# Channel attention into a SwiGLU block: one set of q and k buffers, five of six pairs of d_ff tiles by 7 products, the gate product cut in two, batch 1's softmax spread out

## The chip, the cores and the metric

The kernel runs on one core of a Trainium2 chip. The metric is the device time of one execution in microseconds (us), the median of the runs. The core has five engines that work side by side: TensorE (PE in the profile; its weight loads are PEld), VectorE (DVE), ScalarE (ACT), GpSimd (POOL) and SyncE (SP), which here only issues DMA transfers. Each works through its own instructions in the order in which they were written. A profile was taken of one execution.

## The reference

```python
def _attn_ref(q, k, v, tau):                 # q, k, v: (2, 6016, 256) fp32
    qn = q / (np.linalg.norm(q, axis=1, keepdims=True) + 1e-06)
    kn = k / (np.linalg.norm(k, axis=1, keepdims=True) + 1e-06)
    s = kn.transpose(0, 2, 1) @ qn / tau     # (2, 256, 256)
    s = s - s.max(-1, keepdims=True)
    a = np.exp(s)
    a /= a.sum(-1, keepdims=True) + 1e-09
    return v @ a

def _moe_ref(x, w_gate, w_val, w_out, rms_g):    # x: (12032, 256); weights fp64; d_ff = 1536
    rms = np.sqrt(np.mean(x * x, axis=-1, keepdims=True) + 1e-06)
    xn = x / rms * rms_g
    g = xn @ w_gate
    silu = g * (1.0 / (1.0 + np.exp(-g)))
    val = xn @ w_val
    return silu * val @ w_out
```

The result of the attention, both batches one below the other, is the x of the second function.

## The kernel before

Rows are worked on in tiles of 128. A batch has 47 of them. `scores` multiplies k's tile by q's for the 256 x 256 score matrix; `squares` (ScalarE) squares both, `add_squares` (VectorE) adds the squares up in `acc`, and at the end `join_squares` and `norm_sums` make the column norms of it. Batch 0 goes through this first, chunk by chunk. The `raw` pool holds the chunks of q and k: for batch 0 four buffers of 4 tiles, then, in a pool opened anew, five buffers of 2 tiles for batch 1's 24 chunks. `load_qk` issues two transfers for a chunk on SP, as soon as the chunk that had the buffer before has been squared.

After batch 0's softmax come 24 blocks of up to 4 row tiles, 512 rows (blocks 11 and 23 have 3 tiles, 384 rows; blocks 0 to 11 are batch 0's, 12 to 23 batch 1's). A block j runs through 12 steps f, one for each tile of d_ff, 128 wide; the text writes (j, f) for a step. Every fp32 operand is kept as a high and a low part, and a product is three matmuls: high by high, high by low, low by high.

- A **plain** step (`emit_hidden`) makes gate and value of one d_ff tile with 12 matmuls of 512 columns: six for the gate (`pg`), six for the value (`pv`). ScalarE takes the sigmoid (L629), VectorE multiplies it by the gate (L632, which frees the gate's PSUM bank) and by the value (L639).
- A step by **7 products** (`emit_pair`) works on a pair p = f // 2 of d_ff tiles: halves of the rows and of the 256 inputs are combined as in Strassen's scheme, and one half of the pair's hidden values comes from 7 products of 3 matmuls of 256 columns, 21 in all. The 7 products stand in four PSUM banks. ScalarE copies the first (L580), VectorE adds up the others (L588 to L591). The second step of a pair then takes the sigmoid of both gates (L585, ScalarE), multiplies it by the gates on GpSimd (L586, 1024 columns) and by the values there too (L600, twice 512 columns).

Either way the hidden values are then rounded to a high part on ScalarE (`run_rounds`, L539) and their low part is a subtraction (`run_subs`, L545): on GpSimd for a plain tile, on VectorE for a pair. `emit_out` multiplies the hidden tile by w_out, two steps later in blocks 0 and 1 and three later from block 2 on: 12 matmuls of 256 columns (po) that close each step on TensorE. All products share four PSUM banks (the pool `ps_gv`).

Blocks 0 and 1 are plain throughout (`WINO = 2`). From block 2 on the pairs in `PLAIN` are plain and the others go by 7 products:

```python
PLAIN = (0, 4)
SP = [p for p in range(NP) if p not in PLAIN]
```

Block 0 does two more things. Its steps decode the fp64 weights into fp32 (`decode_w`, `split_w`, three operations of 768 columns a tile on VectorE), and they are filled up with batch 1's scores and squares (`fill`, `square`, `add`; the function `more` calls them with 2 chunks in steps 0 to 4, 1 in the others). `end_block_0` closes that and makes batch 1's norms. Block 1 builds the combined weights for the 7 products (`build_s`, three pieces for a pair, all in the pair's second step).

While block j runs, the activations of block j + 1 are made in its steps, by the table `ready`: v's pieces are transposed in step 0 and split in step 1, multiplied by the softmax in steps 2 and 3, normalized in 4 and 5; at the end of step 5 `emit_xT_move` transposes in VectorE and issues 16 transfers on SP that complete the transposition; `emit_xT_parts` in step 8 scales what lands (L476, ScalarE) and makes the sums for the 7 products (L482, VectorE), and `emit_xT_round` in steps 9 and 10 rounds them (L492). Within a step the order on each engine is the order of the code: the step's own work, then `ready`, then `extra`, the list that `at(j, f, ...)` fills. Batch 1's softmax stands in `extra` at steps 5 to 9 of block 10:

```python
at(B1 - 2, 5 + i, go)
```

## Time and profile before

| | |
|---|---|
| median of 3 runs | 1377.85 us (1377.44 to 1380.14) |
| profiled execution | 1377.68 us, span 1375.9 us |
| mean granted clock of TensorE | 0.981 of full speed |
| TensorE busy | 1322.1 us (96%), 9420 matmuls |
| VectorE busy | 1013.4 us (74%) |
| ScalarE busy | 645.9 us (47%) |
| GpSimd busy | 677.2 us (49%) |

The span is the profiled execution from its first to its last recorded instruction. Busy times are sums over the whole span, whose stages differ: batch 0's scores, the softmax between the phases, block 0 with its extra work, block 1, and the blocks after them.

### The profile page before, as it was taken

The page shows a single profiled execution, that of the slowest core. Times are in us where ns is not written, and L with a number is a line of the kernel's source. Part 1 is how long each engine was busy: PE and PEld are TensorE (multiplying, and loading weights), DVE is VectorE, ACT ScalarE, POOL GpSimd, SP SyncE. Part 2 cuts the span into 40 slices and gives each one's busy share as a digit, 9 for nine tenths or more (in the row PEclk, how much of TensorE's full clock was granted, in tenths as well). Part 3 has the DMA queues.
Part 4 walks back from the last instruction along what each step waited for, and adds up shares of the span by engine and source line. Part 5 has one row for each costly group of instructions (what it writes and reads, how often), then busy time and mean ns, then how long its engine had stood idle before and what let it go on. Part 6 is the DMA issues. An engine that isn't in the chain of part 4 may idle for free.

```text
span 1375.9 us, 24750 instructions
## 1 busy us (share of the span) xinstructions
PE 1322.1 (96%) x9420; PEld 1244.3 (90%) x9420; DVE 1013.4 (74%) x1597; ACT 645.9 (47%) x1244; POOL 677.2 (49%) x500
## 2 busy tenths in 40 slices
...
DMA packets 150870, 71.61 MB, mean 52 GB/s; under 512 B 109280, under 2 KB 136928, under 8 KB 150752
## 3 DMA queue, kind: packets, MB, share of 16 engines
...
q8 instruction: 74, 1.21, 0.4%
...
## 4 chain that ended last, share of the span: by engine, by line
PE 85%; DVE 7%; DMA 2%; ACT 2%; issue 1%; SPq 1%; POOL 0%; DVEq 0%; ACTq 0%; POOLq 0%
PE p L568 31%; PE po L659 26%; PE pg L618 9%; PE pv L618 9%; PE s L175 5%; PE px L377 5%; DMA raw<-in_k_dram 2%; DVE acc L197 1%; DVE wx L120 1%; DVE hh L639 1%; SPq L461 1%; DVE wk L521 1%; DVE th L632 0%; ACT sq L188 0%; DMA raw<-in_q_dram 0%
## 5 line engine op out<-in xcount | busy, mean ns | idle before, releaser
L659 PE MATMUL po<-w,gh 128*128 128x256 f32 x2256 | 409.3, 280 | 0.7 <-ACT gh L539 0.7
L659 PEld LDWEIGHTS po<-w,gh 128*128 128x128 f32 x2256 | 352.1, 188 | 10.0 <-ACT gh L539 1.1
L586 POOL TENSOR_TENSOR th<-th,z 128x1024 f32<-128x1024 f32 (+1 forms) x88 | 207.2, 2354 | 226.4 <-ACT th L585 225.9
L659 PE MATMUL po<-w,gl 128*128 128x256 f32 x1128 | 314.9, 279 | 1.4 <-DVE gl L545 1.4
L568 PE MATMUL p<-xt,w 128*128 128x256 f32 (+1 forms) x2112 | 311.2, 282 | 4.8 <-DVE z L632 4.1
L568 PEld LDWEIGHTS p<-xt,w 128*128 128x128 f32 x2112 | 276.5, 190 | 5.9 <-DVE z L632 4.5
L545 POOL TENSOR_TENSOR gl<-z,gh 128x512 fp32r<-128x512 f32 (+1 forms) x88 | 119.3, 1355 | 240.8 <-ACT gh L539 230.1
L600 POOL TENSOR_TENSOR z<-th,z 128x512 f32<-128x512 f32 (+1 forms) x176 | 220.1, 1272 | 12.2 <-DVE z L591 6.9
L568 PE MATMUL p<-xt,s 128*128 128x256 f32 (+1 forms) x1584 | 217.9, 282 | 2.6 <-DVE z L632 2.3
L659 PEld LDWEIGHTS po<-w,gl 128*128 128x128 f32 x1128 | 212.1, 188 | 1.8 <-DVE gl L545 1.8
L539 ACT ACTIVATE gh<-z 128x512 fp32r<-128x512 f32 (+1 forms) x264 | 163.3, 619 | 88.3 <-POOL z L600 78.5
L568 PEld LDWEIGHTS p<-xt,s 128*128 128x128 f32 x1584 | 200.0, 189 | 4.0 <-DVE z L632 3.2
L588 DVE TENSOR_TENSOR z<-p,z 128x512 f32<-128x512 f32 (+1 forms) x176 | 119.4, 678 | 105.2 <-PE p L568 102.0
L618 PE MATMUL pg<-xt,w 128*128 128x512 f32 (+1 forms) x672 | 178.4, 401 | 4.3 <-DVE th L632 3.5
L618 PE MATMUL pv<-xt,w 128*128 128x512 f32 (+1 forms) x672 | 173.4, 393 | 0.0
L580 ACT ACTIVATE z<-p 128x256 f32<-128x256 f32 (+1 forms) x176 | 66.7, 379 | 201.2 <-PE p L568 197.2
L618 PEld LDWEIGHTS pv<-xt,w 128*128 128x128 f32 x672 | 126.9, 189 | 29.4
L618 PEld LDWEIGHTS pg<-xt,w 128*128 128x128 f32 x672 | 120.2, 190 | 26.4 <-DVE th L632 4.8
L591 DVE TENSOR_TENSOR z<-p,z 128x512 f32<-128x512 f32 (+1 forms) x176 | 119.6, 680 | 19.4 <-DVE z L590 1.4
L589 DVE TENSOR_TENSOR z<-p,z 128x512 f32<-128x512 f32 (+1 forms) x176 | 119.6, 680 | 18.3
L629 ACT ACTIVATE z<-pg 128x512 f32<-128x512 f32 (+1 forms) x88 | 51.4, 584 | 161.9 <-PE pg L618 161.3
L545 DVE TENSOR_TENSOR gl<-z,gh 128x512 fp32r<-128x512 f32 (+1 forms) x176 | 117.8, 702 | 5.9 <-ACT gh L539 5.0
...
## 6 DMA issues: line engine op xcount, KB each, us to landing
...
```

Source lines behind the costliest of these rows:

```text
L175: nc.tensor.matmul(out=s_ps[b][:, c, :], lhsT=r[:, 1, t, c * P:(c + 1) * P], rhs=r[:, 0, t, :], start=(t0 + t == 0 and c == 0), stop=(t0 + ...
L377: nc.tensor.matmul(out=px[:, i, :], lhsT=w[:, c, t * P:(t + 1) * P], rhs=x[:, c, :], start=(i == 0 and c == 0 and m == 0), stop=(c == KC - ...
L539: nc.scalar.activation(out=gh, in_=hh, func=AF.Copy)
L545: engine.tensor_tensor(out=gl, in0=hh, in1=f32(gh), op=ALU.subtract)
L568: nc.tensor.matmul(out=t[:, i, :h], lhsT=wm[wi], rhs=xm[xi], start=(i == 0 and q == 0), stop=(q == 2), skip_group_check=True,)
L586: nc.gpsimd.tensor_tensor(out=th[:, :2 * n], in0=th[:, :2 * n], in1=zg[:, :2 * n], op=ALU.mult)
L588: nc.vector.tensor_tensor(out=zz[:, 0:5:4], in0=ps[1], in1=twice(zz[:, 3:4]), op=ALU.add)
L589: nc.vector.tensor_tensor(out=zz[:, 1:3], in0=ps[2], in1=twice(zz[:, 4:5]), op=ALU.add)
L591: nc.vector.tensor_tensor(out=zz[:, 1:3], in0=ps[3], in1=zz[:, 1:3], op=ALU.add)
L600: nc.gpsimd.tensor_tensor(out=o, in0=i0, in1=i1, op=ALU.mult)
L618: nc.tensor.matmul(out=t[:, :n], lhsT=wgv[wi][:, f, c, wj, :], rhs=x[xi][:, c, :n], start=(m == 0), stop=(m == 3 * KC - 1),)
L659: nc.tensor.matmul(out=o_ps[j][t // 2][:, t % 2, :], lhsT=g[:, t * P:(t + 1) * P], rhs=wo[w][:, f, :], start=(f == 0 and t % 2 == 0 and m ...
```

## The change

- **Buffers.** One `raw` pool of three 4-tile buffers serves both batches; batch 1 comes in 11 chunks of 4 tiles and one of 3. `seq` lists all chunks, and `load_next` issues the next one wherever a chunk has been used up. Batch 1's scores and squares go by parts of 2 tiles; the square of a chunk's second part is written to the output buffer `ob`. The `h` buffers of the plain blocks are one of each instead of two. A step of block 0 fills 2 parts when f is odd, 1 when it is even.
- **Pairs.** `PLAIN = (5,)`: one pair is plain, the last, instead of the first and the fifth. The combined weights of five pairs are built, three pieces one step apart; the first sums of each (two of 512 columns) go to GpSimd.
- **Gate product.** GpSimd's product of 1024 columns is two of 512.
- **Batch 1's norms and softmax.** The end of the sums moves from (0, 11) to (1, 0) and (1, 1), the softmax from steps 5 to 9 of block 10 to single steps of blocks 4 to 7 and two of block 10. v's load for block 1 moves behind step 0 of block 0.

```diff
-    PLAIN = (0, 4)
+    PLAIN = (5,)
...
-    for b, sizes in enumerate(([2] + [4] * 9 + [2] * 4 + [1], [2] * 23 + [1])):
+    for b, sizes in enumerate(([2] + [4] * 9 + [2] * 4 + [1], [CH] * 11 + [3])):
...
-    def squares(b, i):
-
-        n = chunks[b][i][1]
-        sq = pool["sq"].tile([P, 2, n, C], F32, tag="sq", name=f"sq_{b}_{i}")
-        nc.scalar.activation(out=sq, in_=raw[b, i], func=AF.Square)
+    def squares(b, i, t=0, n=None):
+
+        n = n or chunks[b][i][1]
+
+        p, tag = (o_p, "ob") if b and t else (pool["sq"], "sq")
+        sq = p.tile([P, 2, n, C], F32, tag=tag, name=f"sq_{b}_{i}_{t}")
+        nc.scalar.activation(out=sq, in_=raw[b, i][:, :, t:t + n, :], func=AF.Square)
         return sq
...
-        at = [[wgv[0][:, f, c].rearrange("p j m -> p (j m)") for c in range(KC)] for f in (f0, f1)]
         if piece == 0:
-            t = pool["wk"].tile([P, 8, 2 * P], F32, tag="wk", name=f"wk_{p}")
+            t = pool["wk"].tile([P, 4, 2 * P], F32, tag="wk", name=f"wk_{p}")
             s_tmp[p] = t
             for i, f in enumerate((f0, f1)):
-                nc.vector.tensor_tensor(
+                nc.gpsimd.tensor_tensor(
                     out=t[:, 2 * i:2 * i + 2].rearrange("p i n -> p (i n)"),
                     in0=f32(w_hl[0][:, f, :KC * 2 * P]), in1=f32(w_hl[1][:, f, :KC * 2 * P]), op=ALU.add,
                 )
+
         t = s_tmp[p]
-        w11, w12, w21, w22, s1, s2, s3, s4 = (t[:, i] for i in range(8))
         q = SP.index(p)
+        hi, lo = ((x[:, q, :2], x[:, q, 2], w[:, f1, :2 * P]) for x, w in zip(s_hl, w_hl))
+        src = (t[:, 2:4], t[:, 0], t[:, 1])
         if piece == 1:
             for o, i0, i1, op in (
-                (s1, w21, w22, ALU.add), (s2, s1, w11, ALU.subtract),
-                (s3, w11, w21, ALU.subtract), (s4, w12, s2, ALU.subtract),
+                (3, 2, 3, ALU.add), (2, 0, 2, ALU.subtract),
+                (0, 3, 0, ALU.subtract), (1, 1, 0, ALU.subtract),
             ):
-                nc.vector.tensor_tensor(out=o, in0=i0, in1=i1, op=op)
-            nc.scalar.activation(out=s_hl[0][:, q], in_=t[:, 4:7], func=AF.Copy)
-            nc.scalar.activation(out=w_hl[0][:, f1, :2 * P], in_=s4, func=AF.Copy)
+                nc.vector.tensor_tensor(out=t[:, o], in0=t[:, i0], in1=t[:, i1], op=op)
         if piece == 2:
-            nc.vector.tensor_tensor(
-                out=s_hl[1][:, q], in0=t[:, 4:7], in1=f32(s_hl[0][:, q]), op=ALU.subtract
-            )
-            nc.vector.tensor_tensor(
-                out=w_hl[1][:, f1, :2 * P], in0=s4, in1=f32(w_hl[0][:, f1, :2 * P]), op=ALU.subtract
-            )
+            for o, x in zip(hi, src):
+                nc.scalar.activation(out=o, in_=x, func=AF.Copy)
+            for o, x, y in zip(lo, src, hi):
+                nc.vector.tensor_tensor(out=o, in0=x, in1=f32(y), op=ALU.subtract)
...
-            nc.gpsimd.tensor_tensor(out=th[:, :2 * n], in0=th[:, :2 * n], in1=zg[:, :2 * n], op=ALU.mult)
+            for i in range(2):
+                y = slice(i * n, (i + 1) * n)
+                nc.gpsimd.tensor_tensor(out=th[:, y], in0=th[:, y], in1=zg[:, y], op=ALU.mult)
...
-        RAW = 4
-        open_pools(raw=RAW, sq=2, acc=1)
+        RAW = 3
+        seq = [(b, i) for b in range(B) for i in range(len(chunks[b]))]
+
+        def load_next():
+            if seq:
+                load_qk(*seq.pop(0))
+
+        open_pools(both, raw=RAW)
+        open_pools(sq=2, acc=1)
         for i in range(RAW):
-            load_qk(0, i)
+            load_next()
...
-        RAW = 5
-        open_pools(plain, "right", h=2)
-        open_pools(raw=RAW, sq=1, acc=1, wraw=2, wtmp=2)
+        open_pools(sq=1, acc=1, wraw=2, wtmp=2, h=1)
         load_w(0)
-        load_qk(1, 0)
-        load_qk(1, 1)
-        load_qk(1, 2)
         load_w(1)
-        load_qk(1, 3)
-        load_qk(1, 4)
-        new_acc(1, 2)
-        nch = len(chunks[1])
-        filled = [0, 0]
-        waiting = []
+        parts = [(i, t, min(2, n - t)) for i, (_, n) in enumerate(chunks[1]) for t in range(0, n, 2)]
+        to_score, to_square, waiting = list(parts), list(parts), []
 
         def fill(n=1):
-            for i in range(filled[0], min(filled[0] + n, nch)):
-                scores(1, i)
-            filled[0] = min(filled[0] + n, nch)
+            for _ in range(min(n, len(to_score))):
+                scores(1, *to_score.pop(0))
 
         def square(n=1):
-            for i in range(filled[1], min(filled[1] + n, nch)):
-                waiting.append(squares(1, i))
-                raw.pop((1, i))
-                if i + RAW < nch:
-                    load_qk(1, i + RAW)
-            filled[1] = min(filled[1] + n, nch)
+            for _ in range(min(n, len(to_square))):
+                i, t, m = to_square.pop(0)
+                waiting.append(squares(1, i, t, m))
+                if t + m == chunks[1][i][1]:
+                    load_next()
 
         def add(n=1):
             for _ in range(min(n, len(waiting))):
                 add_squares(1, waiting.pop(0))
 
         norms(0)
...
-            n = 2 if f < 5 else 1
+            n = 2 if f % 2 else 1
...
+        at(0, 0, lambda: load_v(1))
...
+        at(0, NF - 1, lambda: (square(24), add(24)))
+        at(1, 0, lambda: join_squares(1, 1))
+        at(1, 1, end_scores)
         for p in SP:
             for i in range(3):
-                at(1, 2 * p + 1, lambda p=p, i=i: build_s(p, i))
-        at(1, NF - 1, end_block_1)
-        for i, go in enumerate((
-            lambda: inverse_norms(1),
-            lambda: spread_norms(1, ps_m, "m"),
-            lambda: (softmax_exp(1, 0), softmax_exp(1, 1)),
-            lambda: softmax_div(1, 0),
-            lambda: softmax_div(1, 1),
-        )):
-            at(B1 - 2, 5 + i, go)
+                f = 2 * p + 1 + i
+                at(1 + f // NF, f % NF, lambda p=p, i=i: build_s(p, i))
+        at(4, 6, lambda: inverse_norms(1))
+        at(4, 7, lambda: spread_norms(1, ps_m, "m"))
+        at(4, 8, lambda: keep_norms(1))
+        at(5, 7, lambda: softmax_min(1, 0))
+        at(6, 7, lambda: softmax_min(1, 1))
+        at(7, 7, lambda: (softmax_exp(1, 0), softmax_exp(1, 1)))
+        at(B1 - 2, 6, lambda: softmax_div(1, 0))
+        at(B1 - 2, 7, lambda: softmax_div(1, 1))
```

On SP's queue, where batch 0's last chunk is loaded (raw_14 is its 15th and last chunk, wraw the fp64 weights of a d_ff tile, the raw_0 after it batch 1's first chunk), before:

```order
L161 DMA raw_14_312<-in_q_dram 128x256
L161 DMA raw_14_312<-in_k_dram 128x256
L97 DMA wraw_372<-in_moe_w_gate_dram 128x2x256
L97 DMA wraw_372<-in_moe_w_val_dram 128x2x256
L101 DMA wraw_372<-in_moe_w_out_dram 128x512
L161 DMA raw_0_376<-in_q_dram 128x512
L161 DMA raw_0_376<-in_k_dram 128x512
L161 DMA raw_1_379<-in_q_dram 128x512
L161 DMA raw_1_379<-in_k_dram 128x512
L161 DMA raw_2_382<-in_q_dram 128x512
L161 DMA raw_2_382<-in_k_dram 128x512
```

and after the change:

```order
L161 DMA raw_14_319<-in_q_dram 128x256
L161 DMA raw_14_319<-in_k_dram 128x256
L161 DMA raw_0_329<-in_q_dram 128x1024
L161 DMA raw_0_329<-in_k_dram 128x1024
L161 DMA raw_1_339<-in_q_dram 128x1024
L161 DMA raw_1_339<-in_k_dram 128x1024
L161 DMA raw_2_346<-in_q_dram 128x1024
L161 DMA raw_2_346<-in_k_dram 128x1024
L97 DMA wraw_377<-in_moe_w_gate_dram 128x2x256
L97 DMA wraw_377<-in_moe_w_val_dram 128x2x256
L101 DMA wraw_377<-in_moe_w_out_dram 128x512
```

Three chunks of 4 tiles now stand directly behind batch 0's last one, ahead of all weights; before, the first weights stood ahead of three chunks of 2 tiles.

On ScalarE, steps 8 to 10 of block 5 (z0_5_4 is what the first step of the fifth pair of block 5 leaves, gh the rounded hidden tiles, xnT_6 and xt0_6 the next block's activations), before:

```order
L629 ACTIVATE z0_5_4_4284<-pg_5_8_4270 128x512
L539 ACTIVATE gh_5_6_4254<-z0_5_3_4196 128x512
L539 ACTIVATE gh_5_7_4256<-z0_5_3_4196 128x512
L476 ACTIVATE xnT_6_4154<-xnT_6_4154,g_sb_99 128x512 x2
L629 ACTIVATE z1_5_4_4329<-pg_5_9_4315 128x512
L539 ACTIVATE gh_5_8_4290<-z0_5_4_4284 128x512
L492 ACTIVATE xt0_6_4306<-xnT_6_4154 128x512 x2
L580 ACTIVATE z0_5_5_4378<-p1_5_10_4353 128x256
L539 ACTIVATE gh_5_9_4334<-z1_5_4_4329 128x512
L492 ACTIVATE xt0_6_4306<-xp_6_4308 128x512 x2
```

and after the change:

```order
L586 ACTIVATE z0_5_4_4422<-p1_5_8_4397 128x256
L545 ACTIVATE gh_5_6_4379<-z0_5_3_4320 128x512
L545 ACTIVATE gh_5_7_4381<-z0_5_3_4320 128x512
L485 ACTIVATE xnT_6_4278<-xnT_6_4278,g_sb_99 128x512 x2
L586 ACTIVATE z1_5_4_4478<-p1_5_9_4453 128x256
L591 ACTIVATE th_5_4_4480<-z0_5_4_4422 128x1024
L501 ACTIVATE xt0_6_4444<-xnT_6_4278 128x512 x2
L637 ACTIVATE z0_5_5_4524<-pg_5_10_4510 128x512
L545 ACTIVATE gh_5_8_4490<-z0_5_4_4422 128x512
L545 ACTIVATE gh_5_9_4492<-z0_5_4_4422 128x512
L501 ACTIVATE xt0_6_4444<-xp_6_4446 128x512 x2
```

The scaling of the next block's activations (L476, now L485) stood ahead of a plain sigmoid of step 9 (z1_5_4 from pg_5_9); now it stands ahead of the copy of step 9's first product (z1_5_4 from p1_5_9) and of the pair's sigmoid, and the sigmoids of the plain steps 10 and 11 come after these.

On VectorE, ahead of block 0's first gate product (th_0_0 by pg_0_0; wx is the decoding of the weights of d_ff tiles 1 and 2), before:

```order
L111 TENSOR_SCALAR wx_1_553<-wraw_1_385 128x768
L120 SCALAR_TENSOR_TENSOR wx_1_553<-wraw_1_385,wx_1_553 128x768
L127 SCALAR_TENSOR_TENSOR wx_1_553<-we_1_555,wx_1_553 128x768
L197 TENSOR_TENSOR acc_1_395<-acc_1_395,sq_1_3_568 128x1024
L111 TENSOR_SCALAR wx_2_576<-wraw_2_503 128x768
L120 SCALAR_TENSOR_TENSOR wx_2_576<-wraw_2_503,wx_2_576 128x768
L127 SCALAR_TENSOR_TENSOR wx_2_576<-we_2_578,wx_2_576 128x768
L632 TENSOR_TENSOR th_0_0_600<-th_0_0_600,pg_0_0_586 128x512
```

and after the change:

```order
L111 TENSOR_SCALAR wx_1_542<-wraw_1_381 128x768
L120 SCALAR_TENSOR_TENSOR wx_1_542<-wraw_1_381,wx_1_542 128x768
L127 SCALAR_TENSOR_TENSOR wx_1_542<-we_1_544,wx_1_542 128x768
L199 TENSOR_TENSOR acc_1_388<-acc_1_388,sq_1_1_2_537 128x1024
L199 TENSOR_TENSOR acc_1_388<-acc_1_388,sq_1_2_0_555 128x1024
L111 TENSOR_SCALAR wx_2_558<-wraw_2_492 128x768
L120 SCALAR_TENSOR_TENSOR wx_2_558<-wraw_2_492,wx_2_558 128x768
L127 SCALAR_TENSOR_TENSOR wx_2_558<-we_2_560,wx_2_558 128x768
L199 TENSOR_TENSOR acc_1_388<-acc_1_388,sq_1_2_2_568 128x1024
L199 TENSOR_TENSOR acc_1_388<-acc_1_388,sq_1_3_0_573 128x1024
L640 TENSOR_TENSOR th_0_0_591<-th_0_0_591,pg_0_0_577 128x512
```

Four additions of squares stand among the decoding there now, where one stood.

## Rows read from the trace of the kernel before

**Rows 1.** windows: us; PE, PEld, DVE, ACT, POOL busy; PEclk; DMA; GB/s

```profile
53.54:78.91 25.37, 18.49 (x91) 15.92 (x91) 12.48 (x28) 11.56 (x26) 7.00 (x6) 0.87 0.78 260
78.91:190.73 111.82, 87.86 (x436) 75.07 (x437) 91.53 (x88) 57.85 (x86) 52.72 (x29) 0.89 0.50 146
190.73:307.14 116.41, 110.09 (x686) 98.94 (x686) 81.09 (x132) 50.02 (x101) 43.68 (x35) 0.95 0.13 28
307.14:664.30 357.16, 357.16 (x2690) 341.16 (x2689) 269.40 (x441) 170.64 (x343) 192.17 (x141) 1.00 0.15 32
664.30:720.50 56.20, 52.56 (x382) 48.75 (x381) 45.65 (x80) 26.88 (x53) 26.64 (x21) 1.00 0.13 27
720.50:1325.54 605.04, 602.76 (x4569) 577.95 (x4567) 455.30 (x760) 287.92 (x585) 326.56 (x241) 1.00 0.15 31
```

**Rows 2.** timeline, PE, blocks 0 and 1: start, us, instruction, [idle before]

```profile
91.52 3.75 PE L175 MATMUL s<-raw 128*128 128x256 f32 x8 [7.48 <-DMA raw<-in_k_dram]
...
113.45 5.77 PE L175 MATMUL s<-raw 128*128 128x256 f32 x16 [6.79 <-DMA raw<-in_k_dram]
...
189.03 1.84 PE L215 MATMUL pn<-ones,acc 128*128 128x1 f32 x8 [8.56 <-DVE acc L202]
190.73 2.91 PE L618 MATMUL pg<-xt,w 128*128 128x512 f32 x6
```

**Rows 3.** timeline, PE, block 9: starts of steps 5, 6, 9, 10, 11

```profile
636.08 0.88 PE L568 MATMUL p<-xt,w 128*128 128x256 f32 x6
...
639.98 0.88 PE L568 MATMUL p<-xt,w 128*128 128x256 f32 x6
...
651.99 1.57 PE L618 MATMUL pg<-xt,w 128*128 128x512 f32 x6
...
656.19 0.88 PE L568 MATMUL p<-xt,w 128*128 128x256 f32 x6
...
660.40 0.88 PE L568 MATMUL p<-xt,w 128*128 128x256 f32 x6
```

**Rows 4.** timeline of DVE, block 9, step 5

```profile
636.17 1.28 DVE L545 TENSOR_TENSOR gl<-z,gh 128x512 fp32r<-128x512 f32 x2
637.41 0.69 DVE L588 TENSOR_TENSOR z<-p,z 128x512 f32<-128x512 f32 x1
...
640.07 1.30 DVE L454 STREAM_TRANSPOSE xw<-xn 128x512 f32<-128x512 f32 x2
```

**Rows 5.** timeline, SP, ACT, DVE, block 9, steps 6 to 9

```profile
641.43 11.48 SPq L461 DMA_DIRECT2D xnT<-xw  x16
...
654.28 1.34 ACT L476 ACTIVATE xnT<-xnT,g_sb 128x512 f32<-128x512 f32 x2 [2.68 <-DMA xnT<-xw]
...
656.66 0.68 DVE L632 TENSOR_TENSOR z<-z,pg 128x512 f32<-128x512 f32 x1
```

**Rows 6.** groups of POOL by line and form: busy, mean ns, idle before

```profile
L600 POOL TENSOR_TENSOR z<-th,z 128x512 f32<-128x512 f32 x160 | 204.2, 1298 | 10.9 <-DVE z L591 6.2
L586 POOL TENSOR_TENSOR th<-th,z 128x1024 f32<-128x1024 f32 x80 | 192.4, 2405 | 206.1 <-ACT th L585 205.6
```

**Rows 7.** timeline of PE and DVE, blocks 1 and 2

```profile
226.22 1.55 DVE L521 TENSOR_TENSOR wk<-wk 128x256 f32<-128x256 f32 x4
...
256.21 2.52 DVE L521 TENSOR_TENSOR wk<-wk 128x256 f32<-128x256 f32 x4
...
261.25 1.80 PE L568 MATMUL p<-xt,w 128*128 128x256 f32 x6 [2.58 <-DVE z L632]
```

**Rows 8.** timeline, DVE, block 0, steps 0, 8 and 9

```profile
87.54 0.68 DVE L632 TENSOR_TENSOR th<-th,pg 128x512 f32<-128x512 f32 x1
...
139.87 0.68 DVE L632 TENSOR_TENSOR th<-th,pg 128x512 f32<-128x512 f32 x1
...
145.40 1.21 DVE L197 TENSOR_TENSOR acc<-acc,sq 128x1024 f32<-128x1024 f32 x1
146.54 0.68 DVE L632 TENSOR_TENSOR th<-th,pg 128x512 f32<-128x512 f32 x1
```

102 lines of the change are left out of this document (54 added, 48 removed).

## The prediction

> **What bounds the kernel now.** I read the stages first, then the spacing of TensorE's steps, then who ends its waits. By stage [rows 1], TensorE is busy without a gap and at clock 1.00 in blocks 3 to 9 (357.16 of 357.16 us) and all but so in blocks 11 to 22 (602.76 of 605.04). There its own work is the bound: a block takes 357.16 / 7 = 51.02 us, and only fewer or cheaper matmuls can shorten it. The stages around them lose time. In the stretch between the two phases TensorE is busy for 18.49 of 25.37 us, in block 0 for 87.86 of 111.82 at clock 0.89, in blocks 1 and 2 for 110.09 of 116.41 at 0.95, in block 10 for 52.56 of 56.20. The long waits are two for q and k data in block 0 (7.48 and 6.79 us) and one of 8.56 us at its end, for the last sum of squares on VectorE [rows 2]. After that one, the six gate matmuls take 2.91 us where they take 1.57 in the steady part [rows 2, 3].
>
> **The matmuls.** A step of the steady part is one d_ff tile's products and one tile's output matmuls. A step by 7 products takes 639.98 - 636.08 = 3.90 us, a plain one 656.19 - 651.99 = 4.20 [rows 3]. One plain pair less per block is two steps, 0.60 us. In the two blocks of 3 tiles I count nothing (bounds 0.6 us to either side, for the same step with a shorter moving side).
>
> **What could eat these 0.60 us.** A step by 7 products needs four operations of VectorE (640.07 - 637.41 = 2.66 us) and per pair two subtractions (637.41 - 636.17 = 1.24) [rows 4]; a plain step needs two of 0.68 us [rows 5]. So VectorE gets 2 x 2.66 + 1.24 - 4 x 0.68 = 3.84 us more per block, on 269.40 / 7 = 38.5 now: 42.3 of 50.4 us, 84%. GpSimd is at 192.17 / 7 = 27.5 us. A pair costs it 2.41 + 2 x 1.30 us [rows 6] and a plain pair two subtractions, which I price like its 1.30 us products; cutting the gate product adds 2 x 1.30 - 2.41 = 0.19 us in each of five pairs. That makes 27.5 + 5.0 - 2.6 + 0.95 = 30.9 us. Neither is full, so no engine takes over the bound on the average.
>
> The order within a block matters more. The plain pair now ends the block; steps 8 and 9, which were plain, become a pair just where the next block's transposed activations arrive. In the shown block SP issues them from 641.43 us for 11.48 us, ScalarE starts to scale them at 654.28, 18.20 us after step 5 began at 636.08, and VectorE is free of the sums behind them at 656.66, 2.38 us after that [rows 3, 5]. Before, what stood behind this on ScalarE was a plain sigmoid. Now it is the copy of the first product of step 9, which frees the PSUM bank that step 10's gate matmuls want, and on VectorE the first sum of step 9, which frees the bank of step 10's second group. Step 10 will start at 5 x 3.90 = 19.50 us after step 5. The copy ends about 18.20 + 1.34 (two scalings) + 0.4 (half the size of one of them) = 19.9. The first sum ends about 18.20 + 2.38 + 0.69 = 21.3; step 10's second group starts at 19.50 + 1.40 = 20.9 (half of a plain step's 4.20 without its twelve output matmuls at 3.90 / 33 = 0.118). By either, this block would wait 0.4 us. It already waits 660.40 - 656.19 - 3.90 = 0.31 there [rows 3], for VectorE's release of step 9's gate product. So I take 0.05 us more on average, a saving of 0.55 per block (bounds: 0.90 if the wait goes altogether, -0.60 if each block waits 1.2 more). Eighteen blocks (3 to 9, 12 to 22): 9.9 us.
>
> **Block 10.** It took 56.20 us, where 51.02 less six x products of a 3-tile successor (0.118 us each) would be 50.3: the batch 1 softmax costs 5.9 us in one block. Spread over blocks 4 to 7 and 10 the same operations fall one at a time; steps 3, 7 and 11 have VectorE time to spare (2.66 of 3.90 in step 7). The norms' inverse at step 6 has no such cover, as step 6 already holds 2.66 + 1.24. I leave 2.0 us of waits (bounds 0 and 5.9). With the 0.55: 4.45 us.
>
> **Blocks 1 and 2.** The 6.3 us of idle TensorE come from pieces of the s weights, all three of a pair in one step: in block 2 TensorE waits 2.58 us for VectorE, whose four sums took 2.52 us just before [rows 7]. Now the pieces are a step apart, and the first sums run on GpSimd (10 of about 1.3 us [rows 6], in a block where GpSimd has room: 43.68 us busy of 116.41 for two blocks). Clock 0.95 over 116.41 us means the lower of the two levels (1.2 of 2.4 GHz) for a tenth of it, 5.8 us lost. The last sum of squares no longer stands ahead of block 1, so most of that goes. I take 4.3 us of idle, 4.1 of clock and 0.6 for block 2's second pair: 9.0 us (bounds 4 and 12).
> The Trainium skill (Perfetto Trace Analysis, Optimizing Scalar/DVE Operations) speaks against this part: it says that GpSimd and VectorE share a read port of SBUF, so that moving work between them may not help. The trace agrees that they disturb each other: the same four sums took 1.55 us at one place and 2.52 at another [rows 7]. By that rule all five pairs would cost VectorE 2.5 us and none 1.55, 5 us more over block 1, which it has to spare there; the sum stays.
>
> **Batch 0's end and block 0.** With one set of buffers, batch 1's first three chunks are issued behind batch 0's last ones, ahead of the weights, so the gap ahead of block 0 shrinks. I expect TensorE's block 0 to begin some 1.5 us earlier, not more: three 4-tile buffers instead of four may cost batch 0 up to 3 us, and the softmax chain needs the same operations. The raw data then comes ahead of need: 24 KB of prefetch instead of 20, the early demand of two parts per step spread to one and two in turn. The two waits of 14.3 us should go. What remains is VectorE's queue. Three more additions of squares stand ahead of the first gate product now, so I put it at 90 us instead of 87.54 [rows 8]. A step with one addition takes 146.54 - 139.87 = 6.67 us, of which the addition is 146.54 - 145.40 = 1.14 [rows 8]; so 5.53 without. Steps 0 to 8 hold 13 additions: 9 x 5.53 + 13 x 1.14 = 64.6, with v's transposes and two scaled subtractions (some 2.1) 66.7. Step 9's gate product is then at 156.7, and TensorE's last step (4.20 and the last part) ends at 162.5. TensorE's own work needs 87.86 us less its half-speed share, close to the same, and two engines that are nearly full cost each other something: I take 165 for the start of block 1, where it is 190.73 now [rows 2]: 25.7 us (bounds 20 and 33).
>
> **The sum**, against the profiled execution: 25.7 + 9.0 + 9.9 + 4.45 = 49.1, so 1377.68 - 49.1 = 1328.6 us, say 1328.5. Its time is within 0.2 us of the median of the runs, 1377.85, so nothing is added.
>
> **Rivals.**
> First, the landing takes the saving back: each block waits some 0.6 us more at step 10, as ScalarE's copy and VectorE's sum of step 9 stand behind the transfer. For it speaks that the margin is a few tenths of a us; against, that landings vary and this block's is a late one. 18 x 0.6 = 10.8, so 1339 (up to 1350 at 1.2).
> Second, block 0 stays hungry: raw loads stand in SP's queue behind weights that wait for VectorE, so the two waits of 14.3 us stay, 1343. Against it: the chunks for steps 1 to 3 are issued before step 0.
> Third, everything hides: block 1 starts at 158, blocks 1 and 2 wait for nothing, the landing wait is gone: 49.1 + 7 + 3 + 2.7 gives 1316.
> Fourth, slower: VectorE becomes the bound in the steady part, through operations stretched by GpSimd. Some 20 of its operations per block read both sides from SBUF, 12.4 us. Stretched by 2.52 / 1.55 = 1.63 [rows 7] they add 7.8, 50.1 of 50.4 us: just full. To lose all 49.1 us, 18 blocks must each be 2.7 us longer than 50.4, a VectorE load of 53.1, a stretch of 1.9 on every one of them: from there on it is slower, 1378 and up. Against it: these operations take 0.62 us each in the steady part [rows 4] though GpSimd is busy half the time.
>
> **Chances.** Forecast (1319 to 1337) 0.55; landing 0.17; hungry block 0 0.12; all hides 0.08; VectorE the bound 0.08, of which 0.05 is slower and 0.03 within 0.2%. A measurement of this kernel tells about 0.2% (2.8 us) from no change; all other cases are faster: 0.92. The range 1311 to 1348 holds the forecast, most of the first three rivals and leaves out the fourth and the tail of the first; alone, the forecast's bounds are 1319 to 1337.
>
> **What would show it.** A 4-tile block from 3 to 9 at 50.3 to 50.5 us, with 0 to 0.5 us of wait in step 10 on ScalarE's copy or VectorE's sum; block 1's first gate matmuls near 165 us, at full speed; no wait of TensorE for raw over 2 us in block 0, and VectorE over 90% busy there; block 10 at 50 to 51 us. The prediction is wrong if block 0's steps take over 7.5 us each, if steady blocks stay at 51, or if the first gate product of block 0 comes after 93 us.

## The result and the profile after

The changed kernel takes 1364.45 us (median of 4 runs, 1363.43 to 1365.35) against 1377.64 us for the kernel before in the same comparison: a ratio of 0.990, 95% interval 0.9883 to 0.9917. That is 13 us faster, where 49 were forecast, and outside the range. The profiled execution took 1363.93 us, its span is 1362.1 us.

By stage, in the changed kernel (the windows end at the first product of block 0, 1, 3, 10, 11 and 23; columns as in [rows 1]):

```profile
0.00:74.90 74.90, 67.42 (x306) 56.92 (x306) 43.01 (x48) 36.96 (x45) 11.36 (x18) 0.95 0.81 260
74.90:174.36 99.46, 85.84 (x428) 72.36 (x429) 86.72 (x86) 56.82 (x86) 50.55 (x29) 0.95 0.55 164
174.36:291.90 117.54, 109.99 (x713) 99.64 (x711) 91.08 (x144) 51.73 (x111) 61.24 (x52) 0.94 0.13 28
291.90:652.20 360.30, 357.35 (x2818) 345.79 (x2817) 311.41 (x493) 177.74 (x359) 223.03 (x182) 1.00 0.15 32
652.20:706.30 54.10, 51.17 (x399) 48.84 (x398) 49.40 (x78) 23.61 (x49) 31.34 (x26) 1.00 0.14 28
706.30:1312.80 606.50, 602.09 (x4784) 585.22 (x4783) 515.92 (x829) 293.47 (x598) 374.45 (x312) 1.00 0.15 31
1312.80:1362.10 49.30, 44.76 (x380) 44.56 (x378) 29.84 (x59) 15.88 (x33) 24.28 (x24) 1.00 0.08 20
```

Against the windows of before:

| stage | before, us | after, us | forecast gain | measured gain |
|---|---|---|---|---|
| up to block 1 | 190.73 | 174.36 | 25.7 | 16.4 |
| blocks 1 and 2 | 116.41 | 117.54 | 9.0 | -1.1 |
| blocks 3 to 9 | 357.16 | 360.30 | 3.85 | -3.1 |
| block 10 | 56.20 | 54.10 | 4.45 | 2.1 |
| blocks 11 to 22 | 605.04 | 606.50 | 6.05 | -1.5 |
| block 23 | 50.36 | 49.30 | 0 | 1.1 |
| sum | 1375.90 | 1362.10 | 49.05 | 13.8 |

The stages that were TensorE's own work became longer, though two steps of each block have fewer matmul columns. VectorE's busy time there rose by 6.0 us a block (311.41 - 269.40, by 7), not by 3.84. Where a block loses it shows in its steps. Their mean lengths over the sixteen blocks 3 to 9 and 13 to 21, each worked out from the starts of first products in TensorE's timeline (names of kernels as in the experiments below):

| step | 0 | 1 | 2 | 3 | 4 to 7, each | 8 | 9 | 10 | 11 | block |
|---|---|---|---|---|---|---|---|---|---|---|
| before | 4.20 | 4.21 | 5.33 | 5.33 | 3.90 | 4.21 | 4.21 | 4.00 | 3.90 | 50.99 |
| after | 4.11 | 3.90 | 5.33 | 5.33 | 3.90 | 3.92 | 4.04 | 4.28 | 4.71 | 51.25 |
| e2_plain4 | 3.90 | 3.90 | 5.34 | 5.91 | 3.90 | 4.22 | 4.21 | 3.96 | 3.90 | 50.96 |
| e3_parts9 | 5.24 | 3.90 | 5.33 | 5.33 | 3.90 | 3.92 | 3.90 | 4.21 | 4.63 | 52.08 |
| e5_plain4_ob | 3.90 | 3.90 | 5.34 | 5.33 | 3.90 | 4.22 | 4.21 | 4.02 | 3.90 | 50.44 |
| e11_ground | 8.05 | 4.02 | 5.33 | 5.33 | 3.90 | 3.92 | 4.06 | 4.29 | 4.26 | 54.88 |

By the shortest steps in the table, a block without any wait would take 50.89 us before and 50.29 after. So 0.60 us was there to be had, and 0.96 us of waits a block took it and more: 0.14 in step 9, 0.07 in step 10, 0.50 in step 11 and 0.21 in step 0. Steps 9 to 11 of block 8, from the timeline of the changed kernel:

```profile
590.58 1.34 ACT L485 ACTIVATE xnT<-xnT,g_sb 128x512 f32<-128x512 f32 x2 [2.48 <-DMA xnT<-xw]
...
591.82 0.36 ACT L586 ACTIVATE z<-p 128x256 f32<-128x256 f32 x1
...
593.27 2.55 POOL L594 TENSOR_TENSOR th<-th,z 128x512 f32<-128x512 f32 x2 [5.84 <-ACT th L591]
...
595.61 2.46 DVE L503 TENSOR_TENSOR xt<-xnT,xt 128x512 fp32r<-128x512 f32 x2
595.84 3.38 POOL L608 TENSOR_TENSOR z<-th,z 128x512 f32<-128x512 f32 x2
...
597.99 0.68 DVE L640 TENSOR_TENSOR z<-z,pg 128x512 f32<-128x512 f32 x1
...
599.38 1.29 DVE L551 TENSOR_TENSOR gl<-z,gh 128x512 fp32r<-128x512 f32 x2
...
600.12 0.39 PE L667 MATMUL po<-w,gl 128*128 128x256 f32 x1 [0.31 <-DVE gl L551]
...
600.58 1.29 DVE L503 TENSOR_TENSOR xt<-xp,xt 128x512 fp32r<-128x512 f32 x2
```

Read it downwards. ScalarE waits 2.48 us for the landing, and the copy of step 9's first product (L586) stands behind that wait. Then the two low parts of the first rounding (L503) take 2.46 us on VectorE, while GpSimd's products with the values (L608) run beside them and take 3.38 us. The second rounding's pair of L503 takes 1.29 us five microseconds later, with no such product beside it. It is so in each block, as the groups of VectorE in blocks 3 to 9 show, by line and form (L351 is the split of v in step 1, L597 one of the sums of the products, with one operand in PSUM; busy, mean ns):

```profile
L351 DVE TENSOR_TENSOR vt<-vw,vt 128x512 fp32r<-128x512 f32 x14 | 18.9, 1391 | 0.0
L503 DVE TENSOR_TENSOR xt<-xnT,xt 128x512 fp32r<-128x512 f32 x14 | 17.7, 1300 | 0.0
L503 DVE TENSOR_TENSOR xt<-xp,xt 128x512 fp32r<-128x512 f32 x15 | 9.7, 686 | 0.0
L597 DVE TENSOR_TENSOR z<-p,z 128x512 f32<-128x512 f32 x70 | 48.4, 692 | 7.6 <-DVE z L596 0.5
```

The same split of v and first rounding in blocks 3 to 9 of the kernel before:

```profile
L342 DVE TENSOR_TENSOR vt<-vw,vt 128x512 fp32r<-128x512 f32 x14 | 10.5, 790 | 0.0
L494 DVE TENSOR_TENSOR xt<-xnT,xt 128x512 fp32r<-128x512 f32 x14 | 9.0, 685 | 0.0
```

The sums with an operand in PSUM are not lengthened: by the timeline, 54 of the 70 of L597 have an operation of GpSimd beside them for over nine tenths of their time, and all take 691 to 693 ns. So it is VectorE's operations with both operands in SBUF that GpSimd's products stretch. Behind the first rounding stand step 10's products with gate and value, behind those the low parts (L551) of the hidden tile of step 8, and for these the output matmuls of step 11 wait.

Two places lose time in the early stages. In block 0 v's load for block 1 now stands on SP behind q and k, and VectorE waits for it (timeline of SP and VectorE):

```profile
92.36 0.36 SPq L161 DMA_DIRECT2D raw<-in_q_dram  x1
92.77 0.43 SPq L161 DMA_DIRECT2D raw<-in_k_dram  x1
93.25 8.45 SPq L336 DMA_DIRECT2D v<-in_v_dram  x4
...
97.58 1.87 DVE L127 SCALAR_TENSOR_TENSOR wx<-we,wx 128x768 uint32<-128x768 uint32 x1
104.73 1.30 DVE L368 STREAM_TRANSPOSE vw<-v 128x512 f32<-128x512 f32 x2 [5.29 <-DMA v<-in_v_dram]
```

TensorE's waits in blocks 0 to 2, and the score matmuls of step 9 of block 0 (timeline of PE; they answer to [rows 2] and to the last row of [rows 7]):

```profile
109.21 2.90 PE L626 MATMUL pg<-xt,w 128*128 128x512 f32 x6 [5.05 <-DVE th L640]
...
159.62 0.63 PE L451 MATMUL pxt<-ident,xn 128*128 128x128 f32 x4 [2.86 <-DVE xt L357]
160.09 3.62 PE L175 MATMUL s<-raw 128*128 128x256 f32 x16
...
231.95 0.62 PE L574 MATMUL p<-xt,w 128*128 128x256 f32 x3 [1.45 <-DVE z L640]
...
235.79 0.79 PE L574 MATMUL p<-xt,s 128*128 128x256 f32 x2 [1.28 <-DVE xt L503]
...
238.70 1.65 PE L574 MATMUL p<-xt,s 128*128 128x256 f32 x6 [2.12 <-DVE z L640]
```

No wait for q and k is left. The wait for the last sum of squares is gone too. In their place stand one behind v's load, one for the bank of the transposes at 159.62, and a row of them in block 2's first step, which goes by 7 products now. During the first wait and in block 2's first step the clock fell (windows around the first wait, and of block 2's first step with the start of the second; PEclk is the third column from the right):

```profile
104.90:114.90 10.00, 5.69 (x21) 4.71 (x22) 9.79 (x10) 4.63 (x7) 4.02 (x3) 0.66 0.88 250
```

```profile
231.95:243.20 11.25, 6.95 (x25) 5.32 (x25) 8.50 (x13) 4.57 (x10) 4.52 (x4) 0.54 0.00 0
```

### The profile page after: what moved, and what is told of

Its sections match the earlier page's. It is cut to its first block, busy times and chain, and to the rows that moved or that the text cites. A ratio compares the mean times of both kernels' runs of the same rounds, so it can differ in the third digit from the quotient of the medians.

```text
span 1362.1 us, 25996 instructions
## 1 busy us (share of the span) xinstructions
PE 1318.6 (97%) x9816; PEld 1253.3 (92%) x9816; DVE 1127.4 (83%) x1732; ACT 656.2 (48%) x1273; POOL 776.3 (57%) x642
## 4 chain that ended last, share of the span: by engine, by line
PE 51%; DVE 24%; SPq 12%; issue 5%; DMA 3%; ACT 3%; POOL 2%; DVEq 0%; ACTq 0%; POOLq 0%
PE p L574 23%; PE po L667 16%; SPq L470 11%; PE px L386 4%; PE s L175 4%; DVE xt L503 3%; DVE z L597 2%; DVE z L599 2%; DVE z L596 2%; DMA xnT<-xw 2%; DVE gl L551 2%; PE pv L626 2%; PE pg L626 2%; DVE z L598 2%; DVE xw L463 1%
## 5 line engine op out<-in xcount | busy, mean ns | idle before, releaser
L594 POOL TENSOR_TENSOR th<-th,z 128x512 f32<-128x512 f32 (+1 forms) x220 | 275.6, 1274 | 304.1 <-ACT th L591 304.0
L574 PE MATMUL p<-xt,w 128*128 128x256 f32 (+1 forms) x2640 | 390.1, 283 | 3.2 <-DVE z L640 1.4
L574 PEld LDWEIGHTS p<-xt,w 128*128 128x128 f32 x2640 | 345.8, 190 | 4.8 <-DVE z L640 1.7
L608 POOL TENSOR_TENSOR z<-th,z 128x512 f32<-128x512 f32 (+1 forms) x220 | 309.6, 1428 | 12.2 <-DVE z L599 10.0
L574 PE MATMUL p<-xt,s 128*128 128x256 f32 (+1 forms) x1980 | 274.6, 283 | 4.4 <-DVE z L640 2.1
L586 ACT ACTIVATE z<-p 128x256 f32<-128x256 f32 (+1 forms) x220 | 83.5, 380 | 264.7 <-PE p L574 264.4
L596 DVE TENSOR_TENSOR z<-p,z 128x512 f32<-128x512 f32 (+1 forms) x220 | 147.9, 672 | 69.0 <-PE p L574 66.2
L597 DVE TENSOR_TENSOR z<-p,z 128x512 f32<-128x512 f32 (+1 forms) x220 | 149.6, 680 | 23.3 <-DVE z L596 0.5
L599 DVE TENSOR_TENSOR z<-p,z 128x512 f32<-128x512 f32 (+1 forms) x220 | 149.5, 680 | 22.9
L551 DVE TENSOR_TENSOR gl<-z,gh 128x512 fp32r<-128x512 f32 (+1 forms) x220 | 139.5, 675 | 0.8 <-ACT gh L545 0.5
L551 POOL TENSOR_TENSOR gl<-z,gh 128x512 fp32r<-128x512 f32 (+1 forms) x54 | 68.7, 1272 | 96.6 <-ACT gh L545 91.0
L626 PE MATMUL pg<-xt,w 128*128 128x512 f32 (+1 forms) x408 | 110.9, 406 | 12.0 <-DVE th L640 5.8
L591 ACT ACTIVATE th<-z 128x1024 f32<-128x1024 f32 (+1 forms) x110 | 114.3, 1039 | 3.5 <-DVE z L599 3.5
L626 PE MATMUL pv<-xt,w 128*128 128x512 f32 (+1 forms) x408 | 106.3, 396 | 1.3 <-DVE z L596 1.3
L598 DVE TENSOR_TENSOR z<-p,z 128x256 f32<-128x256 f32 (+1 forms) x220 | 92.1, 418 | 7.5
```

The source lines that it names most:

```text
L551: engine.tensor_tensor(out=gl, in0=hh, in1=f32(gh), op=ALU.subtract)
L574: nc.tensor.matmul(out=t[:, i, :h], lhsT=wm[wi], rhs=xm[xi], start=(i == 0 and q == 0), stop=(q == 2), skip_group_check=True,)
L594: nc.gpsimd.tensor_tensor(out=th[:, y], in0=th[:, y], in1=zg[:, y], op=ALU.mult)
L596: nc.vector.tensor_tensor(out=zz[:, 0:5:4], in0=ps[1], in1=twice(zz[:, 3:4]), op=ALU.add)
L597: nc.vector.tensor_tensor(out=zz[:, 1:3], in0=ps[2], in1=twice(zz[:, 4:5]), op=ALU.add)
L598: nc.vector.tensor_tensor(out=zz[:, 3], in0=ps[2][:, 0], in1=zz[:, 2], op=ALU.add)
```

## Experiments

All start from the changed kernel. Ratios are to the kernel before, which ran beside each; 0.990 is that of the changed kernel. Ahead of block 0 their code differs at most in the place of v's load, and yet block 0 starts anywhere from 73.7 to 78.0 us, so it is compared by its own length. With the changed kernel's code in it (changed kernel, e2 to e6, e8, e11) block 0 takes 97.7 to 100.4 us, so a difference inside that range says nothing.

### The steady blocks

**e2_plain4** and **e5_plain4_ob**: another pair plain, then also the output copy on ScalarE.

```diff
-    PLAIN = (5,)
+    PLAIN = (4,)
```

> The changed kernel with the fifth pair plain (steps 8 and 9) instead of the sixth (steps 10 and 11); still five pairs by 7 products. Theory: the steady blocks lose their saving because a pair stands at steps 8 and 9, where the next block's activations land; with plain steps there the 4-tile blocks 3 to 9 take 50.3 to 50.6 us instead of 51.5, and the time is 1346 (1342 to 1350). Rival: five pairs load VectorE and GpSimd too much wherever they stand (they stretch each other); then the blocks stay at 51.2 us or more and the time is 1360 to 1366.

Ratio 0.9867 (0.9853 to 0.9882), 1360.28 us; blocks 3 to 9 take 50.92 us each. The blocks lie between the two, and the time at the fast end of the rival's range: the waits of steps 9 to 11 and 0 are all but gone (table), and a new one of 0.6 us stands in step 3. Its rows in block 7 (timeline of VectorE and TensorE):

```profile
508.91 1.28 DVE L551 TENSOR_TENSOR gl<-z,gh 128x512 fp32r<-128x512 f32 x2
510.11 0.68 DVE L679 COPY ob<-po 128x512 f32<-128x512 f32 x1
...
510.94 0.47 PE L667 MATMUL po<-w,gh 128*128 128x256 f32 x2 [0.22 <-ACT xn L402]
```

The first output matmul of a block needs the bank that VectorE's copy of the last block's output frees. The wait is put down to ScalarE, whose operation ended last by the profile, but VectorE's copy ends at 510.79, and the matmul starts 0.15 us later. In e5 ScalarE takes that copy:

```diff
-                if h == 0:
+                if h == 0 and j == NB - 1:
                     nc.vector.tensor_copy(o, o_ps[j][h])
```

> The kernel with the fifth pair plain, and both halves of each block's output copied out of PSUM by ScalarE instead of one half by VectorE. Theory: every 4-tile block still waits 0.5 us in step 3, where the output matmuls want the bank that VectorE's copy frees, and that copy stands behind VectorE's work for two pairs in a row; on ScalarE it comes in time, blocks 3 to 9 take 50.3 us instead of 50.9, and the time is 1349 (1346 to 1352) against 1360.3 with the copy on VectorE. Rival: VectorE is late as a whole, and the wait goes to its next operation in line; then the blocks stay at 50.7 or more and the time is 1357 or more.

Ratio 0.9796 (0.9773 to 0.9819), 1350.46 us. The steady blocks give nearly the whole saving, as the windows of blocks 3 to 9, 10 and 11 to 22 show (of the fastest of the four runs, 1346.09 us):

```profile
289.74:642.31 352.57, 352.57 (x2819) 344.73 (x2817) 296.65 (x486) 182.09 (x364) 217.20 (x183) 1.00 0.15 32
642.31:693.60 51.29, 50.19 (x399) 48.64 (x397) 46.60 (x78) 23.85 (x48) 30.80 (x28) 1.00 0.15 29
693.60:1293.12 599.52, 597.51 (x4784) 584.23 (x4783) 492.35 (x818) 300.57 (x609) 365.65 (x313) 1.00 0.15 31
```

352.57 / 7 = 50.37 us a block, with as many pairs by 7 products as in the changed kernel; by the table's means it is 0.55 us less than before. VectorE is busy for 296.65 us in blocks 3 to 9 instead of 311.41. Of these 14.8 us the copies are 4.8, and the first rounding, which stands beside plain steps again, is 17.7 - 9.1 = 8.6:

```profile
L503 DVE TENSOR_TENSOR xt<-xnT,xt 128x512 fp32r<-128x512 f32 x14 | 9.1, 690 | 0.0
```


**e3_parts9**: scaling and sums of the next block's activations in step 9.

```diff
-            8: (emit_xT_parts,),
-            9: (lambda n: emit_xT_round(n, 0),),
+            9: (emit_xT_parts, lambda n: emit_xT_round(n, 0)),
```

> The changed kernel with the scaling and the sums of the next block's activations one step later, in step 9 instead of 8, ahead of the first rounding. Theory: ScalarE's wait for the landing holds the copy and the sigmoid of step 9 that stand behind it, and so the pair's hidden tiles, which the output matmuls of step 11 want; with the wait behind them the blocks 3 to 9 take 50.4 to 50.8 us and the time is about 1350 (1346 to 1354). Rival: the pair's chain on VectorE and GpSimd is late whatever ScalarE does, and the sums now come later still; then the blocks take 51.3 us or more and the time is 1362 to 1372.

Ratio 1.0007 (0.9998 to 1.0016), 1379.48 us: slower than even the rival's range, and not by its reason. Steps 9 and 10 lost their waits (3.90 and 4.21), so ScalarE's wait for the landing made those. Step 11 keeps its own (4.63). The stretch only moved: the four sums (L491) now stand beside GpSimd's products, and the second rounding beside a subtraction of GpSimd (groups of VectorE in blocks 3 to 9):

```profile
L503 DVE TENSOR_TENSOR xt<-xp,xt 128x512 fp32r<-128x512 f32 x15 | 18.5, 1266 | 0.0
L491 DVE TENSOR_TENSOR xp<-xnT 128x256 f32<-128x256 f32 x14 | 16.9, 1208 | 0.0
L491 DVE TENSOR_TENSOR xp<-xnT,xp 128x256 f32<-128x256 f32 x14 | 13.3, 947 | 0.7
```

In the changed kernel the sums took 423 and 422 ns and the second rounding 686. Behind it stands step 11's gate product (L640), which frees a bank that the next block's first step wants, and that step takes 5.24 us.

**e11_ground**: the low parts of the first rounding on GpSimd.

```diff
-            nc.vector.tensor_tensor(out=o, in0=x, in1=f32(y), op=ALU.subtract)
+            e = nc.gpsimd if i == 0 else nc.vector
+            e.tensor_tensor(out=o, in0=x, in1=f32(y), op=ALU.subtract)
```

> The changed kernel (sixth pair plain) with the low parts of the first rounding of the next block's activations, two subtractions in step 9, on GpSimd instead of VectorE. Theory: these two take 2.46 us on VectorE there, twice their usual time, because GpSimd's products with the values run beside them, and what stands behind them is late: the gate product of step 10 and the low parts of the hidden tiles that the output matmuls of step 11 wait for. Off VectorE, blocks 3 to 9 take 50.3 to 50.8 us instead of 51.4 and the time is 1348 to 1356. Rival: the hidden tiles are late by ScalarE's wait for the landing alone; then the blocks stay at 51.2 us or more and the time is 1361 or more.

Ratio 1.0429 (1.0404 to 1.0453), 1436.37 us: slow as the rival has it, but not by its reason. Step 11 falls from 4.71 to 4.26 us, as the theory wants. But GpSimd reaches the subtractions late, behind its products, and VectorE's second rounding now runs beside them. The next block's first step waits for both (timeline of TensorE, block 8's start; group of the second rounding in blocks 3 to 9):

```profile
570.41 0.50 PE L574 MATMUL p<-xt,w 128*128 128x256 f32 x2 [0.91 <-POOL xt L504]
...
573.24 0.98 PE L574 MATMUL p<-xt,s 128*128 128x256 f32 x6 [1.77 <-DVE z L640]
```

```profile
L504 DVE TENSOR_TENSOR xt<-xp,xt 128x512 fp32r<-128x512 f32 x15 | 25.9, 1762 | 0.0
```

That step takes 8.05 us. That the two low parts make the wait in step 11 is borne out, and the cure is worse. The run takes them off VectorE altogether, so it does not tell their stretch from their plain time.

**e8_whole**: the gate product in one piece.

```diff
-            for i in range(2):
-                y = slice(i * n, (i + 1) * n)
-                nc.gpsimd.tensor_tensor(out=th[:, y], in0=th[:, y], in1=zg[:, y], op=ALU.mult)
+            y = slice(0, 2 * n)
+            nc.gpsimd.tensor_tensor(out=th[:, y], in0=th[:, y], in1=zg[:, y], op=ALU.mult)
```

> The changed kernel with GpSimd's gate product in one piece of 1024 columns again. Theory: the two halves stand one behind the other ahead of the products with the values, so the cut changes only 0.15 us of GpSimd's time per pair; blocks 3 to 9 take 51.3 to 51.6 us and the time is 1362 to 1366. Rival: the cut lets VectorE's operations in between, or costs by its own start; then the blocks differ by 0.3 us or more and the time by 5 us or more.

Ratio 0.9882 (0.9867 to 0.9897), 1361.57 us; a steady block is 51.16 us on the mean against 51.25. The cut gains nothing here, and costs at most 0.1 us a block.

**e6_plain04**: four pairs by 7 products, as before, with the rest of the change.

```diff
-    PLAIN = (5,)
+    PLAIN = (0, 4)
```

> The changed kernel with the first and the fifth pair plain, as before the change; all else of the change stays. Theory: the fifth pair by 7 products costs more than it gives, in the steady blocks and above all at the start of block 2; with four pairs blocks 3 to 9 take 50.9 to 51.0 us, block 3 begins at 285 to 288 us, and the time is 1351 to 1357. Rival: the fifth pair is worth its matmuls, and the rest of the change holds the time up; then it is 1366 to 1373.

Ratio 0.9866 (0.9849 to 0.9882), 1359.21 us, between the two ranges; blocks 3 to 9 take 51.00 us each, block 3 starts at 286.86. The rest of the change by itself is thus worth 18 us, and the fifth pair with the sixth one plain takes 5 of them back. Blocks 1 and 2 take 114.3 us, 3.2 less than in the changed kernel. Steps 0 and 1 of block 2, plain here, take 4.65 and 4.30 us, and step 2, now the first by 7 products, takes 11.45.

### Blocks 1 and 2

**e4_s4late**: the fifth pair's combined weights in block 2.

```diff
-                f = 2 * p + 1 + i
+                f = 2 * p + 1 + i + (6 if p == 4 else 0)
```

> The changed kernel with the combined weights of the fifth pair built in steps 3, 4 and 5 of block 2 instead of steps 9, 10 and 11 of block 1. Theory: the waits around block 2's start come from VectorE's queue, in which the sums for these weights (1.8 us at a time) stand among the roundings and the gate products; without them block 3 begins at 285 to 288 us instead of 291.9 and the time is 1358 to 1361. Rival: block 2's first step goes by 7 products and wants the last rounding of its activations, which comes no earlier; then block 3 begins at 290 or later and the time is 1362 to 1366.

Ratio 0.9899 (0.9883 to 0.9915), 1364.6 us. Blocks 1 and 2 take 117.3 us, no less: steps 0 and 1 of block 2 lost 4.6 us (11.67 instead of 16.31), and steps 6 and 7, behind the moved pieces, gained 5.0 (12.76 instead of 7.80). There TensorE waits for VectorE's sums of the products (1.92 and 1.62 us). The theory named the right queue, and the rival the right time.

**e9_late5**: e5 with v's load moved back (as in e1 below) and the sixth pair's weights in steps 6 to 8 of block 2.

```diff
-                f = 2 * p + 1 + i
+                f = 2 * p + 1 + i + (7 if p == 5 else 0)
```

> The kernel with the fifth pair plain and the output copied by ScalarE, with two more edits: v's load for block 1 at its old place, and the combined weights of the sixth pair built in steps 6, 7 and 8 of block 2, where the steps of VectorE have room, instead of step 11 of block 1 and steps 0 and 1 of block 2. Theory: the waits in block 2's first steps come from VectorE's queue, so the 4.3 us that its step 2 takes too long go, and block 0 ends 2 us earlier; blocks 1 and 2 together take 113 to 115 us instead of 118.0 and the time is 1344 (1341 to 1347). Rival: as when the fifth pair's weights were moved, the wait comes back where the pieces now stand; then blocks 1 and 2 take 117 or more and the time is 1348 to 1351.

Ratio 0.9776 (0.9758 to 0.9793), 1346.96 us, at the slow end of the range. Blocks 1 and 2 take 115.57 us against 117.96 in e5: half of what was expected. Step 2 of block 2 fell from 9.59 to 5.43 us, and step 10, behind the last piece, takes 2.99 us more than its 3.90.

### Block 0

**e1_loadv**: v's load back at its old place.

```diff
-        load_w(3)
+        load_w(3); load_v(1)
         split_w(1)
...
-        at(0, 0, lambda: load_v(1))
```

> The changed kernel with v's load for block 1 back at its old place in the code, behind the load of the fourth d_ff tile's weights. Theory: in block 0 the late v transfers hold VectorE (5.29 us of wait in step 1) and with it TensorE, which then works at the lower clock for a while; without that block 1 begins at 165 to 167 us instead of 174.4, and the time is about 1356 (1354 to 1358). Rival: VectorE's own queue in block 0 sets its end and the wait is made up later; then block 1 begins at 172 or later and the time is 1362 to 1365.

Ratio 0.9897 (0.988 to 0.9913), 1364.41 us. VectorE's wait for v is gone, step 3 takes 9.36 us instead of 14.39. Block 0 gains only half of that: 96.88 us against 99.46, and e9, with the same edit, takes 98.11 against 97.74 in e5. What becomes of the rest shows at step 9 (TensorE's timeline of e9, and the window behind it):

```profile
154.57 1.09 PE L451 MATMUL pxt<-ident,xn 128*128 128x128 f32 x4 [4.43 <-DVE xt L357]
155.45 5.87 PE L175 MATMUL s<-raw 128*128 128x256 f32 x16
```

```profile
155.40:161.00 5.60, 5.60 (x19) 4.58 (x17) 3.87 (x7) 3.25 (x5) 3.10 (x2) 0.59 0.00 0
```

The same place in e1:

```profile
158.32 1.09 PE L451 MATMUL pxt<-ident,xn 128*128 128x128 f32 x4 [2.75 <-DVE xt L357]
159.20 4.56 PE L175 MATMUL s<-raw 128*128 128x256 f32 x16
```

TensorE waits there for the bank of the transposes, which VectorE's queue frees. In e9 it waits 4.43 us, the clock is 0.59 in the window behind that, and the 16 score matmuls that follow take 5.87 us. In e1 it waits 2.75 us, and the 16 take 4.56 us (clock 0.70 over 158.2:163.0). In the changed kernel the wait was 2.86 us, the clock was 1.00 behind it, and the same 16 took 3.62. VectorE's gate product of step 9 comes 3.9 us sooner after the block's start in e1 (81.70 instead of 85.63 us), but from there to the end of the block TensorE needs 15.18 us instead of 13.83 (16.51 in e9), and so gives a part back. Why the clock fell in e1 and not in the changed kernel is open: the two waits are all but equal.

**e7_noadd**: e1 without the 17 additions of squares in block 0's steps.

```diff
                     square()
-                    add()
+                    waiting.clear()
...
-        at(0, NF - 1, lambda: (square(24), add(24)))
+        at(0, NF - 1, lambda: (square(24), waiting.clear()))
```

> The changed kernel with v's load at its old place and without the 17 additions of squares that stand in block 0's steps, so that batch 1's norms hold a part of the rows only. Theory: VectorE's queue, busy for over 95% of block 0, sets its length; without 17 x 1.2 us there block 0 takes 80 to 88 us instead of 96.9. Rival: what holds block 0 is TensorE's own row of waits for ScalarE and GpSimd (the next block's activations, the split weights) and its lower clock; then it takes 92 us or more.

Ratio 0.98 (0.978 to 0.982), 1350.57 us (2 runs). Block 0 takes 84.75 us, 12.1 less than in e1, with the clock at 1.00: VectorE's queue did set its length, down to little more than TensorE's own 81.65 us.

```profile
74.72:159.47 84.75, 81.65 (x428) 69.54 (x429) 68.75 (x70) 57.08 (x86) 49.34 (x29) 1.00 0.64 193
```

**e10_gadd**: e9 with 4 of these additions on GpSimd.

```diff
-                add_squares(1, waiting.pop(0))
+                sq = waiting.pop(0)
+                adds[0] += 1
+                add_squares(1, sq, nc.gpsimd if adds[0] in (9, 12, 15, 18) else nc.vector)
```

> The kernel before this one, and 4 of the 17 additions of squares in block 0's steps go to GpSimd. Theory: VectorE's queue sets block 0, so each addition taken from it saves its 1.2 us: block 0 takes 4 to 5 us less than in the kernel before this one. Rival: an addition on GpSimd reads two operands from SBUF for some 2.5 us, in which VectorE's decoding and additions are stretched by as much, and the next addition waits for it; then block 0 takes as long or up to 3 us longer.

Ratio 0.9815 (0.9796 to 0.9835), 1352.96 us. Block 0 takes 102.44 us, 4.3 more than in e9: the rival, and more. Its groups of additions on VectorE and GpSimd in block 0:

```profile
L199 DVE TENSOR_TENSOR acc<-acc,sq 128x1024 f32<-128x1024 f32 x16 | 28.1, 1755 | 10.5 <-POOL acc L199 7.9 <-ACT sq L190 2.4
```

```profile
L199 POOL TENSOR_TENSOR acc<-acc,sq 128x1024 f32<-128x1024 f32 x4 | 12.4, 3104 | 0.0
```

Sixteen additions cost VectorE as much as the twenty of e9 did (28.1 and 27.9 us), and it waits 7.9 us for GpSimd's.

**e12_fill**: e9 with each step's scores ahead of the work for the next block, and the pieces in steps 5 to 7.

```diff
-            n = j + 1
+            n = j + 1; fill(1 + f % 2) if j == 0 else None
...
             def more(n=n):
-                fill(n)
...
-                f = 2 * p + 1 + i + (7 if p == 5 else 0)
+                f = 2 * p + 1 + i + (6 if p == 5 else 0)
```

> The kernel with the fifth pair plain, the output copied by ScalarE, v's load at its old place and the sixth pair's weights built in block 2 (now in steps 5, 6 and 7), and one edit more: in block 0 each step's scores of batch 1 stand on TensorE ahead of the work for the next block's activations instead of behind it. Theory: at the end of block 0 TensorE waits 4.4 us in step 9 for the bank of the transposes, which VectorE's queue frees late, loses its clock by that, and has 16 score matmuls (3.6 us) left to do afterwards; done ahead of the wait they fill it, so block 0 takes 93 to 95 us instead of 98.1. With the pieces one step earlier the 3 us of wait in step 10 of block 2 go too: blocks 1 and 2 take 113 to 114 us instead of 115.6, and the time is 1341 (1338 to 1344). Rival: VectorE's queue ends no earlier and the last steps wait for it instead; then block 0 takes 97 or more and the time is 1345 to 1348.

Ratio 0.9762 (0.9745 to 0.9779), 1344.78 us. Block 0 takes 92.00 us, 6.1 less than in e9, at clock 1.00, better than expected:

```profile
74.73:166.73 92.00, 82.64 (x429) 69.25 (x429) 86.02 (x84) 55.56 (x84) 50.62 (x28) 1.00 0.60 178
```

VectorE's gate product of step 9 comes no sooner than in e9 (81.62 and 81.60 us after the block's start); the whole gain lies behind it, where TensorE needs 10.38 us instead of 16.51. The second edit failed: blocks 1 and 2 take 119.37 us, 3.8 more, half of it in block 1 (step 10 takes 7.14 us) and half in steps 8 to 10 of block 2. With e9 this is the fastest version that ran: 32 us ahead of the kernel before, and 20 ahead of the changed one by their medians.

## Why the prediction was wrong

- **The matmuls** were right: 0.60 us a block, and e5 gets 0.55 of it.
- **What could eat it** is the step that cost most: 9.9 us forecast for the steady blocks, -4.6 measured (block 11 included). The place was named (the landing meets a pair at steps 8 and 9) and the size missed: "0.05 us more on average" is 0.86 (0.96 of waits a block against 0.10 before). It followed the sums of the activations and left out the two roundings behind them, and it took every duration from the rows of before, where no product of GpSimd ran beside these operations, since steps 8 and 9 were plain. (A subtraction of GpSimd did run beside the first rounding there. It began 0.2 us later, took 1.62 us instead of 1.30, and left VectorE's at 0.68.) And half of the wait (0.50 of 0.96 us) is not for the PSUM banks of step 10 but in step 11, whose output matmuls want the hidden tile of step 8.
- **The stretch that was set aside.** The row that spoke for it was there: 1.55 and 2.52 us for the same four sums [rows 7]. Rival four priced it as a mean over all VectorE's operations and found it just bearable; it works at one place in each block instead. L503 takes 2.46 us beside L608 and 1.29 without; L608 takes 3.38 beside L503, where its two products took 2 x 1.30 before [rows 6]. The Trainium skill (Perfetto Trace Analysis, Optimizing Scalar/DVE Operations) says that moving work between VectorE and GpSimd may not help, since they share a read port; e10 agrees, 4.3 us slower.
- **Block 10**: the cost of the spread softmax was sized rightly, if e5 is asked: 51.29 us there against 51.75 forecast. The changed kernel's 54.10 has waits for VectorE's sums on top: steps 8 to 10 take 16.1 us there against 14.1 in e5, with the softmax's divisions and the next block's sums ahead of them on VectorE and GpSimd's products beside these. With plain steps 8 and 9 it is 51.87 (e6).
- **Blocks 1 and 2**: "most of that goes" failed. The lower clock at block 1's start went (1.00 over its first 15.6 us, where it was 0.81 over the first 14.3), and a lower clock came back at block 2's start. Over both blocks it is 0.94 instead of 0.95, and TensorE is idle for 7.55 us instead of 6.32. The prediction asked where the pieces of the weights had stood, and not what stands at steps 9 to 11 where the last of them come to stand: the sums and roundings for block 2. With its first pair by 7 products, block 2 wants the second rounding at once. e4 and e9 show that VectorE's queue makes the wait and that pieces moved later make one there. The last two steps of block 1 take 5.69 and 5.92 us instead of 4.21 in the changed kernel, and about as long in e4 and e9; the fourth pair's sums stand there behind the sums for block 2, and no run moved these.
- **Block 0**: the price of VectorE's steps was good. From the first gate product (at 87.15, where 90 was forecast) to that of step 9 it forecast 66.7 us; it was 73.4, of which 5.29 are the wait for v. That wait is the first miss: the load's move past q, k and weights on SP was not priced. The second is "TensorE's last step ends at 162.5". TensorE does its instructions in order, and in step 9 it waits for the transposes' bank with 16 score matmuls and two steps still to do; from step 9's gate product on it took 13.83 us, not 5.8, and ended at 174.36. e12 takes those matmuls out from behind the wait and gains 6.1 us.
- **The rivals.** The first, the landing, was the nearest in place, with 0.6 us a block against 0.86. The second did not come: no wait for q and k is left. The fourth had the right mechanism and the wrong measure.
- Right were the waits for q and k, which went, and the start of block 0, 4.0 us earlier in this execution (1.5 forecast), of which a part is luck, as it varies by 4 us from run to run.

What makes the 0.96 us of waits is shown for a good part. Those of steps 9 and 10 (0.21) go with ScalarE's wait for the landing (e3), and 0.45 of step 11's 0.50 with the two low parts on VectorE (e11), though both runs starve the next block's first step instead. The 0.21 of step 0 stand behind the second rounding by the timeline, which no run tested. Open is how much is the stretch: no run has the two low parts at this place without GpSimd's products beside them. As an estimate, the stretch of 2.46 - 1.29 = 1.17 us alone is more than step 11's wait.
